# An earlier load of two head pairs and a later load of w_out in a fused cosine-attention and two-layer kernel

## The chip, the cores and the metric

The kernel runs on one core of a Trainium2 chip. The metric is the device time of one execution in microseconds (us): 413.31 us is the median of three runs of the kernel before the change, which lie between 413.31 and 413.9 us. The times of engines, waits and transfers come from one profiled execution of it, taken by the hardware profiler. The engines are called as in the profile: PE is TensorE (matrix products), DVE is VectorE, ACT is ScalarE, POOL is GpSimd, and SP is SyncE, which here only issues transfers (DMAs). POOL issues transfers too, on a queue of its own.

## What is computed

```python
q_n = q / (norm(q) + 1e-6);  k_n = k / (norm(k) + 1e-6)      # over the 64 channels of a head
attn = softmax(q_n @ k_n^T / tau)                            # per batch and head
o    = attn @ v                                              # q, k, v: [8, 12, 448, 64] float32
x    = o, with the 12 heads of a token side by side          # [3584, 768]
h    = x @ w_in;  g = max(0.01 * h, h)                       # w_in: [768, 2048]
out  = g @ w_out                                             # w_out: [2048, 768], out: [3584, 768]
```

The inputs and the output are float32 in memory; the matrix products run in bf16.

## The kernel before

**Pairs and quads.** Two heads of one batch are a *pair*; there are 6 pairs in a batch and 48 in all, numbered `s` from 0 (so the eleventh pair has number 10, and is called pair 10 here). Two pairs are a *quad* `j`, three in a batch. A pair goes through these steps, each of which is a function of the kernel:

- `load_qk(s)` (lines 135 to 147) issues four transfers on SP: the first 384 rows of q (L140), those of k (L141), and the last 64 rows of each (L143). The six pairs of the first batch have a tensor of their own, `raw0`; later pairs use one of four rotating buffers called `qk` (L139). A load can start only when the buffer's former pair has been read for the last time, which is the normalising of that pair.
- `squares(s)` (L180) squares q and k on POOL, `sums(s)` (L191) adds up each row on DVE, `roots(s)` (L198 and L199) takes the square root on ACT by logarithm and exponential, and `normalise(s)` (L215, L216, L220) divides and rounds to bf16 on DVE, into `qn`.
- `transposes(s)` brings channels onto partitions: by PE and a DVE copy (L258) for pairs 0 to 9, by a transposing DMA on SP (L252) from pair 10.
- `key_tiles` makes a tile of scores on PE (L277) and its exponential on ACT (L289), into `pe`, or `pr` for the 64 rows that are left over. Then `totals`, `products` and `scale` (L317, L336, L337, L358) form the attention output in `xT`.

`norm(s)` calls `roots`, `normalise` and `transposes` of pair `s`, issues the load of a later pair, and then puts `squares(s + 2)` on POOL. Ahead of the squares stands `hold` (L511), a tiny copy on POOL that reads the last part of `qn[s]`; it keeps POOL from going on before pair `s` is normalised.

**The two layers.** `first(c, m)` makes columns `m` of the first layer for a chunk of tokens (L381, 16 values of `m`) and ACT applies the leaky relu while it moves the result from its PSUM bank to `hT` (L388). `firsts(b, ...)` runs over all 16, with parts of the attention's preparation put between them. `visit(b, ...)` then makes the second layer of the same chunk (`groups`, L456) and, between its groups, the score tiles of the next batch, one tile at a time. A group is the two matmuls, on the two halves of the partitions, for one `m`. In the first visit (b = 0) two row tiles are worked on together in four parts of the 16 values of `m`: groups 1 to 16 need the first quarter of `w_out`, 17 to 32 the second, 33 to 48 the third, 49 to 64 the fourth. A second pass of 32 groups follows for the third row tile. The dictionaries `wide`, `three` and `four` say behind which group a score tile stands, and `norms` behind which group a pair's `sums` or `norm` stands.

**Order.** The order of the instructions on each engine is written out by hand: the program's order is the engine's order, and an instruction that waits holds up all that is behind it on its engine. There are eight PSUM banks, dealt out oldest first by `banks`; a matmul that is to write a bank waits until ACT or DVE has emptied it. The two queues that matter here are SP's (q1 in the profile, the loads of q and k, transposing DMAs and stores) and POOL's (q0, the loads of v, `w_in` and `w_out`, which round float32 to bf16 on the way). The weights are loaded in four parts each: `load_w_in(0..3)` (L106) and `load_w_out` (L112) for `m` from 0, 4, 8 and 12. They are issued from `bulk(s)` in the first batch, `w_out` right behind the last part of `w_in` and behind the squares of pair 7.

Around the change the program's order is: the attention of quad 2 (`attend(NQ - 1, ...)`, whose last step is `scale(2, 0)` and `scale(2, 1)` on DVE); `norm(6)` and `norm(7)`; `firsts(0, ...)` with `norm(8)`, `norm(9)`, the loads of v and `norm(10)` between its columns; `visit(0, ...)`, with `sums(11)` and `norm(11)` between its groups; and `attend_batch(1)`, which begins with the loads of pairs 14 and 15.

Of the kernel before, what the change touches and what calls it, by code (L numbers as in the profile page):

```python
# [8 lines left out]
F32 = mybir.dt.float32  # L9
# [7 lines left out]
def kernel(  # L17
# [10 lines left out]
    nc = tc.nc  # L28
    B, H, S, D = q.shape
# [9 lines left out]
    NQ = NPAIR // 2  # L39
# [11 lines left out]
    ldp = ctx.enter_context(tc.tile_pool(name="ld", bufs=4))  # L51
# [36 lines left out]
    def given_back(keep):  # L88
        deals["n"] += 1
        for i in kept.pop(keep):  # L90
            age[i] = deals["n"]
# [18 lines left out]
    def load_w_out(parts):  # L110
        for m in parts:
            gp.dma_start(out=w_out_sb[:, m : m + MT // 4], in_=w_out_r[:, m : m + MT // 4])  # L112

    def main(x, b, h0, nh):
        return x[b, h0 : h0 + nh, 0:MAIN].rearrange("h (p t) d -> p h t d", t=3)

    raw0 = cpool.tile([128, NPAIR, 2, 7, D], F32, name="raw0")
# [17 lines left out]
    def load_qk(s):  # L135
        if s >= NSLOT:
            return
        b, h0 = s // NPAIR, 2 * (s % NPAIR)
        both = ldp.tile([128, 2, 7, D], F32, name="qk")  # L139
        nc.sync.dma_start(out=both[:, :, 0:3], in_=main(q, b, h0, 2))  # L140
        nc.sync.dma_start(out=both[:, :, 4:7], in_=main(k, b, h0, 2))  # L141
        for i, x in enumerate((q, k)):
            nc.sync.dma_start(  # L143
                out=both[64 * i : 64 * i + 64, :, 3],
                in_=x[b, h0 : h0 + 2, MAIN:S].rearrange("h p d -> p h d"),
            )
        raw[s] = (both[:, :, 0:4], both[:, :, 4:7])
# [5 lines left out]
    def load_v(j):  # L153
        if j >= B * NQ:
            return
        b, jj = divmod(j, NQ)
        vb[j] = vbp.tile([128, 4, 3, D], BF16, name="v_b")
        gp.dma_start(out=vb[j], in_=main(v, b, 4 * jj, 4))  # L158
# [12 lines left out]
    def squares(s, engs=(gp, gp)):  # L171
        if s >= NSLOT:
            return
        tiles = []
        for x, eng, name in zip(raw[s], engs, ("sq0", "sq1")):
            sq = sqp.tile(list(x.shape), F32, name=name)
            if eng is nc.scalar:
                nc.scalar.activation(sq, x, func=AF.Square)
            else:
                eng.tensor_tensor(sq, x, x, op=ALU.mult)  # L180
            tiles.append(sq)
        sqs[s] = tiles

    def sums(s, parts=(0, 1)):
        if s >= NSLOT:
            return
        if s not in ss:
            ss[s] = smp.tile([128, 14], F32, name="ss")
        for i in parts:
            o = ss[s][:, 0:8] if i == 0 else ss[s][:, 8:14]  # L190
            nc.vector.tensor_reduce(  # L191
                o.rearrange("p (h t) -> p h t", h=2), sqs[s][i], axis=AX.X, op=ALU.add
            )
# [7 lines left out]
    qn, scalings = {}, {}  # L201

    def behind(eng, ins, why):

        tc.add_manual_dep(
            eng.nop().ins, ins.ins.name,
            mybir.DependencyInfo(mybir.DependencyClass.Sync, mybir.DependencyReason.DATA),
            reason=why,
        )
# [143 lines left out]
    def scale(j, e):  # L353
        b, jj = divmod(j, NQ)
        m, half = divmod(b, 2)
        if m not in xT:
            xT[m] = xtp.tile([128, KT, 2 * S], BF16, name="xT")
        nc.vector.tensor_tensor(  # L358
            xT[m][:, 2 * jj + e, half * S : (half + 1) * S], pos.pop((j, e))[:, :S], rbs[j],
            op=ALU.mult,  # L360
        )
        if (j, e) in kept:
            given_back((j, e))
# [3 lines left out]
    def chunk_cols(c):  # L367
        return (0, MAIN) if c % 2 == 0 else (MAIN, 512)
# [3 lines left out]
    def first(c, m, kts=range(KT)):  # L372

        c0, n = chunk_cols(c)
        if c not in hT:
            hT[c] = htp.tile([128, MT, 512], BF16, name="hT")
        if (c, m) not in pms:
            pms[c, m] = banks(1)
        pm = pms[c, m]
        for kt in kts:  # L380
            nc.tensor.matmul(  # L381
                out=pm[:, :n],
                lhsT=w_in_sb[:, kt, m * 128 : (m + 1) * 128],
                rhs=xT[c // 2][:, kt, c0 : c0 + n],
                start=(kt == 0), stop=(kt == KT - 1),
            )
        if kts[-1] == KT - 1:
            nc.scalar.activation(  # L388
                out=hT[c][:, m, :n], in_=pms.pop((c, m))[:, :n], func=AF.Prelu, alpha=0.01
            )  # L390
            if (c, m, 0) in kept:
                given_back((c, m, 0))
# [160 lines left out]
    def bulk(s):  # L553

        if s == 0:
            load_v(1)
            load_w_in(0)
        elif s == 1:
            load_v_rem(0, slice(2, 4))
            load_w_in(1)  # L560
        elif s == 2:
            load_v(2)
            load_w_in(2)
        elif s == 3:
            load_w_in(3)
            load_w_out((0, 4))
        elif s == 4:
            load_w_out((8, 12))

    def scaled(s):  # L570

# [81 lines left out]
    def attend(j, behind=()):  # L653
        totals(j)
        reciprocals(j)
        po = banks(2)
        for e in range(2):
            products(j, e, po[:, e])
        for fn in behind:
            fn()  # L660
        for e in range(2):
            scale(j, e)
# [30 lines left out]
    def norm(s, transposed=True):  # L693
        if s >= NSLOT:
            return
        roots(s)
        normalise(s)
        if transposed:
            transposes(s)
        if s == 10:  # L700
            return
        if s == 11:
            load_qk(12)
            load_qk(13)
        elif s not in (7, 8):
            load_qk(s + (2 if s == 9 else 4))
        hold(qn[s][:, 6, 0, 0:1])
        if s == 11:
            squares(12)
        squares(s + 2)  # L710

    def firsts(b, begun, between):

# [8 lines left out]
    def visit(b, order, norms, between):  # L722
# [14 lines left out]
        key_tiles([(s0 + 5, 3)])  # L737

    three = ({5: 1, 11: 1, 16: 2, 21: 1, 27: 1}, {3: 1, 7: 1, 11: 1, 16: 2, 20: 1})
    wide = (dict.fromkeys((5, 10, 16, 21, 26, 32, 37, 42, 48, 53, 58, 63), 1), three[1])  # L740
    four = ({5: 1, 11: 1, 16: 2, 24: 1}, {6: 1, 16: 2})

    deals["apart"] = False
    attend(NQ - 1, [lambda m=m: first(0, m, range(KT - 2)) for m in range(3, SOON)])
    norm(6, False)
    norm(7, False)
    firsts(
        0, SOON, {
# [11 lines left out]
    for b in range(B):  # L760
        tokens = chunk_cols(b)[1] // 128
        if b == B - 1:
            for ts in range(tokens):
                for half in range(2):
                    second(b, ts, half)
            break
        order = [[((ts, 0), (ts, 1))] for ts in range(tokens)]
        if b == 0:
            order = [order[0] + order[1], order[2]]
        norms = {(0, 16): [lambda: sums(11)], (0, 26): [lambda: norm(11)]}  # L770
        if b:
            norms = {}
            for i in range(tokens - 1):
                norms[i, 4] = [lambda s=ready + i: norm(s)]
                norms[i, 20] = [lambda s=ready + i + 1: sums(s)]
        visit(b, order, norms, wide if b == 0 else three if tokens == 3 else four)
        ready += tokens - 1
        attend_batch(b + 1)
        for j in range((b + 2) * NQ, (b + 3) * NQ):
            load_v(j)  # L780
        load_v_rem(b + 2)
        s = ready
        between = {0: [lambda s=s: norm(s)], 1: [lambda s=s: sums(s + 1)]}
        if b == 0:
            between = {
                0: [lambda: sums(13)], 1: [lambda: norm(13), lambda: sums(14)],
                4: [lambda: norm(14), lambda: sums(15)], 7: [lambda: norm(15)],
                13: [lambda: sums(16)],
            }
            ready += 4  # L790
        elif tokens == 3:
            between.update({
                4: [lambda s=s: norm(s + 1), lambda s=s: sums(s + 2)],
                7: [lambda s=s: norm(s + 2), lambda s=s: sums(s + 3)],
                10: [lambda s=s: norm(s + 3)], 13: [lambda s=s: sums(s + 4)],
            })
            ready += 4
        else:
            between.update({
                4: [lambda s=s: norm(s + 1)], 5: [lambda s=s: sums(s + 2)],  # L800
                8: [lambda s=s: norm(s + 2)], 12: [lambda s=s: sums(s + 3)],
            })
            ready += 3
        firsts(b + 1, 0, between)
# [35 lines left out]
```

## Time and profile before

| | us |
|---|---|
| device time, median of 3 runs | 413.31 |
| device time of the profiled execution | 413.39 |
| span of its instructions | 411.6 |
| PE busy | 402.1 |
| ACT busy | 263.4 |
| DVE busy | 189.6 |
| POOL busy | 139.0 |

The span is the time from the first to the last instruction on any engine; the 1.8 us between it and the device time lie before and after the instructions. "Busy" is time in which an engine had an instruction of the program in work. The profile cuts the span into 40 slices of 10.3 us each and prints the busy share of each engine as one digit, in tenths; the row PEclk is the clock that PE was granted, in tenths of its full speed. A wait is named as "engine line waited for", with its total, how often, and the longest one. In the rows by window the columns are the window, its length, and for each engine the busy time and the number of instructions, then the granted clock of PE (1.00 is full), the mean busy share of the 16 DMA engines (over 1 when transfers overlap), and GB/s.

### The profile page before, as it was taken

The numbers are of one execution on the slowest core, as the hardware profiler recorded it, in microseconds if no ns is written. First come the engines' busy times: TensorE is split into PE (matmuls) and PEld (weight loads), VectorE is DVE, ScalarE is ACT, GpSimd is POOL, SyncE is SP. The second block draws the span as 40 slices with busy tenths as digits, with TensorE's granted clock in tenths as the row PEclk, the third lists the DMA queues.
The fourth block names the chain that finished last, engine by engine and source line by source line (L and its number), as shares of the span: only waits on it lengthen the run. The fifth ranks groups of instructions, "written<-read, shape, count | busy, mean of one in ns | idle before, by whom it ended". The sixth has DMA issues, their size and how long they took to land.

```text
span 411.6 us, 10137 instructions
## 1 busy us (share of the span) xinstructions
PE 402.1 (98%) x4096; PEld 215.8 (52%) x4096; DVE 189.6 (46%) x405; ACT 263.4 (64%) x454; POOL 139.0 (34%) x212
## 2 busy tenths in 40 slices
PE   8999979999999999999999999999999999999996
PEld 3335546544555555544555555544555555554564
DVE  6887733573542635255352726157261544130021
ACT  4996468744876569845786469855776559844300
POOL 4992244283241514055140634054232530000000
PEclk9999989999999999999999999999999999999999
DMA  7999999599296948386387866575478832210023
GB/s 184 250 214 219 222 157 199 160 178 185 65 167 148 137 114 170 102 115 154 95 187 144 111 141 128 142 99 128 99 176 156 112 90 62 62 41 2 0 77 78
DMA packets 102095, 54.21 MB, mean 132 GB/s; under 512 B 69984, under 2 KB 96992, under 8 KB 102048
## 3 DMA queue, kind: packets, MB, share of 16 engines
q1 hardware_dynamic: 78064, 41.04, 43.4%
q0 software_dynamic: 23136, 12.00, 22.0%
q8 instruction: 32, 0.52, 0.6%
q10 hardware_dynamic: 848, 0.52, 0.4%
q14 instruction: 15, 0.12, 0.1%
HBM read 45.61 MB, written 11.01 MB: 138 GB/s over the span
## 4 chain that ended last, share of the span: by engine, by line
PE 88%; DMA 5%; DVE 2%; POOL 1%; issue 1%; ACT 1%; SPq 1%; POOLq 0%
PE ps L381 32%; PE ps L456 30%; PE ps L317 11%; PE ps L277 8%; PE ps L418 5%; DMA qk<-in_k_dram 3%; DMA raw<-in_q_dram 2%; PE ps L304 1%; DVE qn L220 1%; POOL sq L180 1%; DVE ss L191 0%; DVE r L216 0%; DVE xT L358 0%; ACT pe L289 0%; ACT pr L289 0%
## 5 line engine op out<-in xcount | busy, mean ns | idle before, releaser
L381 PE MATMUL ps<-xT,w_in_sb 128*128 128x384 bf16 (+1 forms) x768 | 148.2, 353 | 0.0
L456 PE MATMUL ps<-w_out_sb,hT 64*128 64x384 bf16 x1536 | 144.8, 325 | 2.1 <-ACT hT L388 2.1
L289 ACT ACTIVATE pe<-ps 128x896 bf16<-128x896 f32 x144 | 124.2, 918 | 21.0 <-PE ps L277 18.8
L388 ACT ACTIVATE hT<-ps 128x384 bf16<-128x384 f32 (+1 forms) x128 | 67.4, 543 | 70.4 <-PE ps L381 70.0
L381 PEld LDWEIGHTS <-w_in_sb 128*128 128x128 bf16 x768 | 74.0, 98 | 71.9 <-issue 4.0
L456 PEld LDWEIGHTS <-hT 64*128 64x128 bf16 x1536 | 75.4, 95 | 57.2 <-issue 5.2
L180 POOL TENSOR_TENSOR sq<-qk 128x512 f32<-128x512 f32 x84 | 77.3, 941 | 20.4 <-DMA qk<-in_k_dram 19.5
L191 DVE TENSOR_REDUCE ss<-sq 128x6 f32<-128x384 f32 (+1 forms) x95 | 54.6, 611 | 8.0 <-POOL sq L180 7.6
L277 PE MATMUL ps<-qkT 64*128 64x448 bf16 (+1 forms) x384 | 55.1, 356 | 2.2 <-ACT pe L289 0.8
L468 DVE COPY osb<-ps 128x384 f32<-128x384 f32 x41 | 21.2, 554 | 73.0 <-PE ps L456 42.5
L511 POOL CAST seen<-qn 128x1 f32<-128x1 bf16 x47 | 8.9, 189 | 130.5 <-DVE qn L220 123.9
L220 DVE TENSOR_TENSOR qn<-qk,r 128x512 bf16<-128x512 f32 x84 | 50.2, 639 | 1.7 <-DVE r L216 0.3
L215 DVE TENSOR_SCALAR ss<-ss 128x14 f32<-128x14 f32 x48 | 10.4, 216 | 68.2 <-ACT ss L199 68.1
L358 DVE TENSOR_TENSOR xT<-ps,rb 128x448 bf16<-128x448 f32 x48 | 27.8, 620 | 26.6 <-ACT rb L337 26.4
L158 POOL DMA_DIRECT2D v_b<-in_v_dram x24 | 18.6, 778 | 54.2 <-PE ps L317 54.2
L317 PE MATMUL ps<-pe,v_b 128*32 128x448 bf16 x576 | 32.0, 353 | 0.0
L277 PEld LDWEIGHTS <-qkT 64*128 64x128 bf16 (+1 forms) x384 | 16.7, 97 | 21.8 <-issue 9.4
L424 DVE COPY osb<-ps 128x384 f32<-128x384 f32 (+1 forms) x9 | 4.6, 514 | 36.5 <-issue 22.6
L336 ACT ACTIVATE rb<-ps 128x448 f32<-128x448 f32 x24 | 12.9, 538 | 13.2 <-PE ps L317 12.3
L317 PEld LDWEIGHTS <-v_b 128*32 128x32 bf16 x576 | 15.1, 97 | 12.0 <-issue 0.6
L289 ACT ACTIVATE pr<-ps 128x896 bf16<-128x896 f32 x24 | 21.2, 918 | 0.2 <-PE ps L277 0.2
L418 PE MATMUL ps<-w_out_sb,hT 128*128 128x384 bf16 (+1 forms) x144 | 21.0, 308 | 0.0
(49 smaller groups left out, 199.6 us busy)
## 6 DMA issues: line engine op xcount, KB each, us to landing
qk<-in_q_dram SPq DMA_DIRECT2D x42, 192.0 KB, 3.3
qk<-in_k_dram SPq DMA_DIRECT2D x42, 192.0 KB, 3.3
out_dram<-osb SPq DMA_DIRECT2D x30, 192.0 KB, 2.9
v_b<-in_v_dram POOLq DMA_DIRECT2D x24, 192.0 KB, 4.7
out_dram<-osb SPq DMA_DIRECT2D x12, 384.0 KB, 2.8
w_in_sb<-in_moe_w_in_dram POOLq DMA_DIRECT2D x4, 768.0 KB, 12.0
w_out_sb<-in_moe_w_out_dram POOLq DMA_DIRECT2D x4, 768.0 KB, 24.9
qk<-in_q_dram SPq DMA_DIRECT2D x42, 32.0 KB, 3.4
```

Source lines behind the costliest of these rows:

```text
L180: eng.tensor_tensor(sq, x, x, op=ALU.mult)
L191: nc.vector.tensor_reduce(o.rearrange("p (h t) -> p h t", h=2), sqs[s][i], axis=AX.X, op=ALU.add)
L220: scalings[s] = nc.vector.tensor_tensor(qn[s][:, lo:hi], x.rearrange("p h t d -> p t h d"), r[:, r0 : r0 + 2 * nt].rearrange("p (h t) -> p ...
L277: nc.tensor.matmul(out=out[:, a, :S], lhsT=x[rows, c0:c1], rhs=x[rows, 0:S], start=True, stop=True,)
L289: nc.scalar.activation(out=dst, in_=sc[:, :, :S], func=AF.Exp, scale=inv_tau)
L317: nc.tensor.matmul(out=x[32 * g : 32 * g + 32, :S], lhsT=weights(g, ki) if ki < 3 else rem(g), rhs=pe[s][:, ki, a, :] if ki < 3 else pr[j] ...
L358: nc.vector.tensor_tensor(xT[m][:, 2 * jj + e, half * S : (half + 1) * S], pos.pop((j, e))[:, :S], rbs[j], op=ALU.mult,)
L381: nc.tensor.matmul(out=pm[:, :n], lhsT=w_in_sb[:, kt, m * 128 : (m + 1) * 128], rhs=xT[c // 2][:, kt, c0 : c0 + n], start=(kt == 0), stop= ...
L388: nc.scalar.activation(out=hT[c][:, m, :n], in_=pms.pop((c, m))[:, :n], func=AF.Prelu, alpha=0.01)
L418: nc.tensor.matmul(out=po2[:, :n], lhsT=hT[c][:, m, ts * 128 : (ts + 1) * 128], rhs=w_out_sb[:, m, lo : lo + n], start=(m == 0), stop=(m = ...
L456: done[p][i] = nc.tensor.matmul(out=pos2[p][:, i, :HALF], lhsT=hT[c][rows, m, ts * 128 : (ts + 1) * 128], rhs=w_out_sb[rows, m, half * HAL ...
L468: copy(out=osb[c, ts][:, half * HALF : (half + 1) * HALF], in_=po2[:, i, :HALF])
```

## The change

Three things move; no operation is added to or taken from the computation.

1. Pairs 10 and 11 are loaded into the places of pairs 0 and 1 in `raw0`, in place of two of the rotating buffers. Both loads are issued on SP behind a wait for the first of the two scalings of quad 2. The loads of pairs 12 and 13 stay at `norm(11)`, and those of 14 and 15 at the attention of the next batch; they now take the rotating buffers of pairs 6 to 9.
2. The four parts of `w_out` leave `bulk`: two are issued by POOL behind the squares of pair 8 and two behind those of pair 9.
3. In the first visit the score tiles stand at other groups (11 in the first pass and 7 in the second, in place of 12 and 6), and `sums(11)` and `norm(11)` stand behind groups 8 and 18 in place of 16 and 26.

```diff
-        both = ldp.tile([128, 2, 7, D], F32, name="qk")
+        both = raw0[:, s - 10] if s in (10, 11) else ldp.tile([128, 2, 7, D], F32, name="qk")
...
-        nc.vector.tensor_tensor(
+        scalings[j, e] = nc.vector.tensor_tensor(
...
             load_w_in(3)
-            load_w_out((0, 4))
-        elif s == 4:
-            load_w_out((8, 12))
...
-        if s == 11:
-            load_qk(12)
-            load_qk(13)
-        elif s not in (7, 8):
-            load_qk(s + (2 if s == 9 else 4))
+        for x in (12, 13) if s == 11 else (s + 4,) if s > 11 else ():
+            load_qk(x)
         hold(qn[s][:, 6, 0, 0:1])
         if s == 11:
             squares(12)
         squares(s + 2)
+        if s in (6, 7):
+            load_w_out((0, 4) if s == 6 else (8, 12))
...
-    wide = (dict.fromkeys((5, 10, 16, 21, 26, 32, 37, 42, 48, 53, 58, 63), 1), three[1])
+    wide = (dict.fromkeys((5, 11, 16, 22, 27, 33, 38, 44, 49, 55, 60), 1), dict.fromkeys(range(4, 29, 4), 1))
...
     attend(NQ - 1, [lambda m=m: first(0, m, range(KT - 2)) for m in range(3, SOON)])
+    behind(nc.sync, scalings[NQ - 1, 0], "weights first")
+    load_qk(10)
+    load_qk(11)
     norm(6, False)
     norm(7, False)
...
-        norms = {(0, 16): [lambda: sums(11)], (0, 26): [lambda: norm(11)]}
+        norms = {(0, 8): [lambda: sums(11)], (0, 18): [lambda: norm(11)]}
```

`behind(engine, instruction, why)` makes the engine wait until that instruction of another engine has ended; `load_qk` and `load_w_out` are as described above.

## The prediction

> **What bounds the kernel now.** I read the page first: PE is busy in all but 9.5 us of the span, so only those microseconds, or a slower PE clock, can be won. In the slices the one hole far from both ends is the sixth digit of PE (51 to 62 us), with a lower PEclk below it.
>
> ```profile
> span 411.6 us, 10137 instructions
> PE 402.1 (98%) x4096; PEld 215.8 (52%) x4096; DVE 189.6 (46%) x405; ACT 263.4 (64%) x454; POOL 139.0 (34%) x212
> PE   8999979999999999999999999999999999999996
> PEclk9999989999999999999999999999999999999999
> ```
>
> PE's waits between 30 and 160 us name the hole; the windows price it. The first window is the first visit, from its first score tile to the next attention (L304); the second is the third visit, which has as many matmuls. The last shows PE's clock at half.
>
> ```profile
> PE ps L456 <- ACT hT L388: 2.1, 1, 2.1
> PE ps L277 <- ACT pr L289: 0.5, 1, 0.5
> PE ps L277 <- ACT pe L289: 0.3, 1, 0.3
> ```
>
> ```profile
> 50.56:75.62 25.06, 22.15 (x249) 13.32 (x256) 7.82 (x17) 19.11 (x26) 12.30 (x17) 0.93 1.02 178
> 150.39:170.32 19.93, 19.93 (x248) 11.20 (x256) 7.44 (x17) 18.35 (x26) 4.78 (x7) 1.00 0.60 121
> ...
> 55.00:56.00 1.00, 1.00 (x8) 0.53 (x6) 0.23 (x1) 1.00 (x2) 0.00 (x0) 0.50 1.17 202
> ```
>
> So the first visit has an excess of 25.06 - 19.93 = 5.13 us: waits of 2.1 + 0.47 + 0.34, and some 2.2 left for the half clock, which follows the wait from about 54.5 to 58.2. The chain that ended last says why ACT was late (start, us, what):
>
> ```profile
> 38.42 0.61 SPq L143
> ...
> 39.07 11.32 DMA qk<-in_k_dram
> ...
> 51.55 0.84 POOL sq L180
> ...
> 52.41 0.56 DVE ss L191
> ...
> 53.00 0.32 ACT ss L198
> 53.32 0.02 issue
> 53.34 0.21 ACT ss L199
> 53.56 0.38 ACT hT L388
> ```
>
> Pair 10's last piece needs 11.32 us to land (50.4); squares, sums and roots follow. The roots stand on ACT ahead of the last relu, whose bank PE needs at 51.88. Last, the transfers. Here are POOL's issues of w_out and its squares (start, us, what), then the packets, MB and engine share of each queue from 42 to 44 us; from 40 to 42 us, nearly without SP's; and from 68 to 69 us, SP's alone.
>
> ```profile
> 26.21 1.52 POOL L112 DMA_DIRECT2D w_out_sb<-in_moe_w_out_dram  x2
> 29.65 1.55 POOL L112 DMA_DIRECT2D w_out_sb<-in_moe_w_out_dram  x2
> 38.13 2.38 POOL L180 TENSOR_TENSOR sq<-qk 128x512 f32<-128x512 f32 x2 [0.38 <-POOL seen L511]
> 41.59 1.82 POOL L180 TENSOR_TENSOR sq<-qk 128x512 f32<-128x512 f32 x2 [0.95 <-DMA qk<-in_k_dram]
> ```
>
> ```profile
> q0 software_dynamic: 210, 0.30, 83.3%
> q1 hardware_dynamic: 211, 0.15, 30.6%
> ...
> q0 software_dynamic: 240, 0.37, 101.0%
> ...
> q1 hardware_dynamic: 380, 0.27, 108.3%
> ```
>
> The queues take turns packet by packet (210 and 211), and POOL's are bigger; so beside weights SP gets 0.075 MB/us, alone 0.27. The weights occupy q0 until about 58 us.
>
> **Part 1, loads 10 and 11 at quad 2's scaling.** In the trace SP issues load 10 at 37.49 (after pair 6's normalising) and load 11 at 39.88. The new wait ends with the scaling that starts at 34.71, at about 35.3: two and four microseconds earlier. By itself that is worth nothing: load 9 has the SP queue until it lands at 41.43, and the order in it stays. Behind the waiting SP instruction stand only these eight issues and then the transposing DMAs of pairs 10 and 11, which before go at 55.39 and 64.08; nobody else waits. The places of pairs 0 and 1 were last read by 20 us. Load 11's last pieces still wait, as before (1.52 us of issue at 41.52), until load 9's pieces have landed. Loads 12 to 15 only get buffers that are free longer.
>
> **Part 2, w_out behind the squares of pairs 8 and 9.** POOL gives back 1.52 us at 26.21 and 1.55 at 29.65; it then waits for pair 6 until 37.56 anyway, so the path gains nothing there. The issues move to 40.5 (end of pair 8's squares) and, with pair 9's squares pushed to 42.2 to 44.1, to 44.1. These squares are summed at 44.88, so the push is covered by 0.8 us. Pair 10's squares can begin at about 45.8. w_in's last part lands at 40.5 (issued 25.40, 15.1 us), and a v load issued at 60.00 has its packets from about 62.0; so for at least 2 us, 40.5 to 42.5, SP has the DMA engines alone. It moves 2 x 0.27 = 0.54 MB, more than load 10's 0.46. Load 10 lands at 43 to 45 in place of 50.4. Load 11, with the rest at 0.075 MB/us, takes (0.92 - 0.54) / 0.075 = 5.1 us more: 48 to 50 in place of 58.1 (53 if SP alone were no faster than half of 0.27).
>
> Then the chain is: squares 45.8 to 47.7; DVE has copies until 49.35 (48.20 + 1.15) and sums pair 10 by 50.7 (1.34); roots 0.56 and relu 0.38 end at 51.6, before PE asks at 51.88. The 2.1 us go, and with them the half clock, 2.2. Next late is the first pr exponential: 0.82 after the relu, 52.4, where PE asks at 52.05. I leave the whole 0.47 wait in.
>
> The price is w_out's arrival. In the trace its parts land at 46.3, 50.6, 55.8 and 59.9 (issues plus 20.1, 23.6, 26.2 and 29.4). PE will need part k at 51.06 + 16k x 0.163 + 0.19 for each score tile passed + 0.45: 51.1, 54.6, 57.7, 60.8. From below: if the engines do the same work in the same time, only in another order, all is there at 59.9 and PE waits 0. From above: the two queues apart need 0.54/0.27 = 2.0 us, then 0.38 MB of loads beside 0.76 of w_out at 0.225 MB/us = 5.1, then the other 2.39 MB at 0.185 = 12.9; 20.0 us where the mix took 4.07/0.225 = 18.1. That is 1.9 late: 61.8; and pair 10's transposing DMA, now ahead of the last part, can add up to 1.5 (143.9% of the engines in the us from 57): 63.3, a wait of 2.5. I take 0.7, nearer the lower end, because the lower end is the row of the same packets and engines.
>
> The page "SBUF — State Buffer" of the Trainium skill (section "SBUF: two separate sides") speaks against the move: descriptors that POOL writes stall while some DVE operations hold a shared port. The trace: w_out's issues at 26 to 31 us took 0.76 us each with DVE busy 1.00, v's at 60.0 0.77 with DVE at 0.5; but a v load landed after 5.7 us at 14.13 and 4.6 at 60.00. By the rule w_out would be 1 us later and the sum 410.4; by the issue rows it is unchanged.
>
> **Part 3, tiles and norm(11).** The number of tiles stays 18, so PE and ACT have the same work. In the steady visits, 18 tiles, three pr and a relu fit ACT (18.35 of 19.93); tiles every four groups in the second pass (4 x 0.163 + 0.19 = 0.84 against 0.86 an exponential) lag by some tenths, covered by the 5.79 us of L317 before the last are read. The 0.34 us wait at 68.3 goes with the wider spacing; if it stays, 0.3 is lost. ACT reaches roots(11) at 51.6 + 5 x 0.87 = 56.0; its sums come 2.6 us after load 11 lands (58.07 to 60.64 before), so at about 53, hidden. The cover is gone from a landing at 53.4 on. norm(11) before the rest only moves loads 12 and 13 ahead (65.4 to about 60); squares 12 wait behind the v loads as before and are read past 75 us.
>
> **Sum**, against the profiled execution's 413.39 (0.08 over the median): 413.39 - 5.13 + 0.47 + 0.7 = 409.43; on the median 409.4.
>
> **Rivals.**
> - *w_out is late by more.* For: its queue starts about 2 us (up to 4) later. Wait of 1.5 to 2.5: 410.2 to 411.2.
> - *Slower: a w_out wait that halves PE's clock again.* At the third or fourth quarter one wait of over about 2 us (2.1 did it; 0.47 did not) costs itself and 2.2 again. With 0.47, it decides at 2.5 us: 5.13 - 0.47 - 2.2. Every us beyond is lost: w_out's last part past 63.3, 3.4 later than before, would do; at 64.3 the wait of 3.5 gives 409.4 + 2.8 + 2.2 = 414.4. Against: that lies past my upper bound. The page "TensorE: Matmul & The Clock Gate" of the Trainium skill (section "What's actually happening") puts the gate at an idle window of about 3.4 us. This trace halves after 2.1, so the measurement decides; by the rule a wait of 3.3 would cost only itself and give 412.0.
> - *The clash moves to roots(11).* If load 11 lands past 53.4, ACT stands at roots(11), 8 groups earlier than before, and the tile at group 33 waits for its bank (0.65 us of slack). At 56 the sums come at 58.6, roots and one exponential 1.4 later, 2.0 after the tile asks: 411.4. Against: SP's time alone.
> - *The change does not do what it says:* no time alone for SP, pair 10 lands at 50 as before: 413.3.
>
> **How the numbers follow.** Forecast (w_out wait below 1.5: 408.2 to 410.2) 0.69; w_out late by more 0.11; roots(11) 0.07, a fifth of it no gain; no effect 0.04; slower 0.09, a little of it within 0.2%. 0.2% (0.8 us) is about what a measurement of this kernel can tell from no change. Faster 0.86, same 0.05, slower 0.09. The range runs from 408.2 (all 5.13 gone, no new wait) to 411.5, the end of the late w_out.
>
> **What would show it.** Right: w_out issued near 40.5 and 44; load 10 landing before 46, load 11 before 53; no L456 wait on hT; PEclk full at 51 to 62 us; the first visit 20 to 22 us. A wait of L456 on w_out is the price. Wrong: L388 still late, a long ACT wait at L198, or a second half-clock stretch.

## The result, and the profile after

The changed kernel takes 409.37 us (median of 4 runs, 408.64 to 409.56) against 413.46 us before (413.31 to 413.9 beside it): a ratio of 0.9896, 95% interval 0.9879 to 0.9913. The forecast was 409.4. The profiled execution took 409.41 us with a span of 407.6. As will be seen, the mechanism was the one forecast, but that the total fits this closely is partly luck: two terms were too high by about 1 us together, and that was made up by 0.6 us and some pauses that stood in no term. One part of the change was judged wrongly.

The page of the changed kernel, the same rows as before: the hole at 51 to 62 us and the clock's dip below it are gone.

```profile
span 407.6 us, 10141 instructions
PE 399.9 (98%) x4096; PEld 215.1 (53%) x4096; DVE 189.6 (47%) x405; ACT 263.1 (65%) x454; POOL 138.7 (34%) x212
PE   7999999999999999999999999999999999999996
PEclk9999999999999999999999999999999999999999
```

PE's waits between 30 and 160 us are down to one, and the windows show the stretch before the visit and the first visit (51.16 to 71.66), each with 0.2 us of idle time of PE left:

```profile
PE ps L277 <- ACT pr L289: 0.2, 1, 0.2
```

```profile
34.94:51.16 16.22, 16.00 (x116) 9.60 (x112) 15.08 (x28) 8.37 (x23) 11.54 (x17) 1.00 1.10 220
51.16:71.66 20.50, 20.33 (x249) 13.00 (x249) 6.39 (x15) 18.70 (x26) 7.91 (x12) 1.00 1.22 209
```

The visit is 25.06 - 20.50 = 4.56 us shorter, and begins 51.16 - 50.56 = 0.60 us later: 3.96 us in all, and the span fell by 4.0. Now the transfers. The first rows are load 10's four pieces in the changed kernel with their time to landing (issued from 35.43 to 37.17, so landed by 42.4, before 50.4); then the packets of the two queues from 40 to 42 us and from 48 to 50 us:

```profile
raw<-in_q_dram SPq DMA_DIRECT2D x1, 192.0 KB, 6.1
raw<-in_k_dram SPq DMA_DIRECT2D x1, 192.0 KB, 6.1
raw<-in_q_dram SPq DMA_DIRECT2D x1, 32.0 KB, 5.7
raw<-in_k_dram SPq DMA_DIRECT2D x1, 32.0 KB, 5.2
...
q1 hardware_dynamic: 806, 0.48, 78.9%
q0 software_dynamic: 12, 0.02, 13.8%
...
q0 software_dynamic: 275, 0.42, 116.0%
```

From 40 to 42 us SP had the engines almost to itself (806 packets, 0.48 MB); from 48 to 50 us w_out had them, and moved 0.42 MB. POOL issued w_out at 39.99 and 43.46 (start, us, what), and the parts landed between 7.8 and 15.1 us after their issue, the last at 59.3:

```profile
39.99 1.56 POOL L112 DMA_DIRECT2D w_out_sb<-in_moe_w_out_dram  x2
...
43.46 1.56 POOL L112 DMA_DIRECT2D w_out_sb<-in_moe_w_out_dram  x2
```

### The profile page after: what moved, and what is told of

Its sections match the earlier page's. It is cut to its first block, busy times and chain, and to the rows that moved or that the text cites. A ratio compares the mean times of both kernels' runs of the same rounds, so it can differ in the third digit from the quotient of the medians.

```text
span 407.6 us, 10141 instructions
## 1 busy us (share of the span) xinstructions
PE 399.9 (98%) x4096; PEld 215.1 (53%) x4096; DVE 189.6 (47%) x405; ACT 263.1 (65%) x454; POOL 138.7 (34%) x212
## 4 chain that ended last, share of the span: by engine, by line
PE 88%; DVE 5%; POOL 2%; ACT 1%; DMA 1%; issue 1%; POOLq 0%
PE ps L381 33%; PE ps L456 31%; PE ps L317 11%; PE ps L277 8%; PE ps L418 5%; DVE qn L220 2%; PE ps L304 1%; POOL sq L180 1%; DMA raw<-in_k_dram 1%; DVE ss L191 1%; DVE ss L215 1%; DVE qkT L258 1%; DVE r L216 0%; POOL raw L130 0%; POOL v_rem L165 0%
## 5 line engine op out<-in xcount | busy, mean ns | idle before, releaser
L180 POOL TENSOR_TENSOR sq<-qk 128x512 f32<-128x512 f32 x80 | 73.4, 938 | 10.7 <-DMA qk<-in_k_dram 10.1
L220 DVE TENSOR_TENSOR qn<-qk,r 128x512 bf16<-128x512 f32 x80 | 48.2, 644 | 1.7 <-DVE r L216 0.3
L215 DVE TENSOR_SCALAR ss<-ss 128x14 f32<-128x14 f32 x48 | 10.5, 220 | 69.2 <-ACT ss L199 69.1
```

What stands on the lines that cost most here:

```text
L220: scalings[s] = nc.vector.tensor_tensor(qn[s][:, lo:hi], x.rearrange("p h t d -> p t h d"), r[:, r0 : r0 + 2 * nt].rearrange("p (h t) -> p ...
```

## The experiments

Three questions were open after the result. Which of the three parts makes the gain? What does the half clock cost, apart from the wait that sets it off? And why does PE enter the first visit 0.6 us later? The theory at the start was the prediction's: the later w_out frees pair 10, the earlier load does nothing by itself, and the moved tiles cost nothing once load 11 is early. In what follows the length of the first visit is taken from the start of its first score tile to the start of the first L304, both from the timeline; it is 24.99 us in the kernel before and 20.43 in the changed one. It leaves out when PE enters the visit, which varies from execution to execution.

### One part at a time

**The later w_out alone** (kernel before plus)

```diff
             load_w_in(3)
-            load_w_out((0, 4))
-        elif s == 4:
-            load_w_out((8, 12))
...
         squares(s + 2)
+        if s in (6, 7):
+            load_w_out((0, 4) if s == 6 else (8, 12))
```

> The kernel before with the later issue of w_out alone; pairs 10 and 11 are loaded as before. Theory (the gap in POOL's queue is what frees pair 10): SP's transfers have the engines alone from about 38.5 to 42.5 us, load 10 lands before 46 us, the wait of L456 on hT and the half clock are gone, and nearly the whole gain is there: 409 to 410.2 us. Rival (the earlier load is needed): load 10 still lands near 50 us and the time stays near 413.4.

Measured: 410.19 us (409.78 to 410.76), ratio 0.9930 (0.9902 to 0.9958). Load 10, issued from 38.30 on, landed by 42.3; the wait on hT and the half clock are gone. The theory held. The time is 0.8 us over that of the full change: the visit takes 20.81 us, and in the profiled run PE entered it 0.4 us later, after a wait of 0.8 us for w_in's last part. A wait of 0.3 for pe stayed, as before.

**The earlier loads alone** (kernel before plus)

```diff
-        both = ldp.tile([128, 2, 7, D], F32, name="qk")
+        both = raw0[:, s - 10] if s in (10, 11) else ldp.tile([128, 2, 7, D], F32, name="qk")
...
+    behind(nc.sync, scalings[NQ - 1, 0], "weights first")
+    load_qk(10)
+    load_qk(11)
     norm(6, False)
```

> The kernel before with the earlier loads of pairs 10 and 11 alone; w_out is issued as before. Theory: load 9 and the weights hold the queues, load 10 lands near 50 us as before, 413 to 413.7 us. Rival (the earlier issue frees pair 10): load 10 lands some 2.4 us earlier, the wait of L456 shrinks below 0.5 us, the clock stays full and the time is 409 to 411.

Measured: 410.52 us (410.38 to 410.75), ratio 0.9936 (0.9915 to 0.9957). The theory fell: this part alone is worth 3.0 us. Its waits of PE, and its packets from 40 to 42 us:

```profile
PE ps L381 <- DMA w_in_sb<-in_moe_w_in_dram: 0.7, 1, 0.7
PE ps L456 <- ACT hT L388: 0.5, 1, 0.5
PE ps L277 <- ACT pr L289: 0.5, 1, 0.5
PE ps L277 <- ACT pe L289: 0.3, 1, 0.3
```

```profile
q0 software_dynamic: 199, 0.30, 82.9%
q1 hardware_dynamic: 203, 0.15, 30.2%
```

In the kernel before, the same 2 us show 240 packets of w_out and only 94 of SP's, and 17 of those in the first of the two: load 9 had all but run out, and load 10, asked for from 37.49 on, was hardly flowing. With the earlier issue SP takes its turn there (203 packets), and load 10 lands at 49.3 in place of 50.4. PE itself came to the visit 0.54 us later, after the wait for w_in, so the 1.1 us were enough to bring its wait on hT from 2.1 to 0.5 us. The clock stayed at 1.00 after that. The waits listed went from 2.1 + 0.47 + 0.34 to 0.5 + 0.5 + 0.3, and the half clock went: the visit took 21.75 us (from 51.10 to 72.85).

**The moved tiles, sums(11) and norm(11) alone** (kernel before plus)

```diff
-    wide = (dict.fromkeys((5, 10, 16, 21, 26, 32, 37, 42, 48, 53, 58, 63), 1), three[1])
+    wide = (dict.fromkeys((5, 11, 16, 22, 27, 33, 38, 44, 49, 55, 60), 1), dict.fromkeys(range(4, 29, 4), 1))
...
-        norms = {(0, 16): [lambda: sums(11)], (0, 26): [lambda: norm(11)]}
+        norms = {(0, 8): [lambda: sums(11)], (0, 18): [lambda: norm(11)]}
```

> The kernel before with the moved score tiles, sums(11) and norm(11) alone. Theory: load 11 lands at 58 us as before, its sums come at 60.6, and ACT now reaches roots(11) some 3 us earlier and stands there; the tiles behind it are late and PE waits 0.5 to 2 us more for pe: 413.8 to 415.5. Rival (ACT's backlog is covered by the two free tile buffers): 413.2 to 413.6, or less by the 0.34 us wait on pe at 68.3.

Measured: 415.22 us (413.12 to 417.37, 10 runs), ratio 1.0038 (1.001 to 1.0066): a little slower, as the theory has it, though the runs scatter widely. In the profiled run, 416.21 us, load 11 landed late, ACT came to roots(11) early and stood there 2.90 us, PE waited 2.1 us for pe, and the clock fell after that second wait. ACT's rows (start, us, what, idle before):

```profile
56.26 2.85 ACT L289 ACTIVATE pe<-ps 128x896 bf16<-128x896 f32 x3
62.01 0.31 ACT L198 ACTIVATE ss<-ss,tiny 128x14 f32<-128x14 f32 x1 [2.90 <-DVE ss L191]
```

```profile
PE ps L456 <- ACT hT L388: 2.2, 1, 2.2
PE ps L277 <- ACT pe L289: 2.1, 1, 2.1
```

**Both other parts, without the moved tiles.** The edits of the first two runs together.

> The changed kernel with the old positions of the tiles, sums(11) and norm(11). Theory: the new positions do little once load 11 is early; 409.2 to 409.9. Rival (the wider spacing is what takes away the waits on pe in the second half of the visit): two or more waits of L277 on pe, 410 to 411.

Measured: 409.88 us (409.85 to 410.38), ratio 0.9924 (0.9897 to 0.9951). This is inside the theory's range, at its upper end. One wait on pe of 0.3 us stays, and the visit takes 20.81 us where the full change takes 20.43. The moved tiles are worth about 0.4 us once load 11 is early.

**The later w_out and the moved tiles, without the earlier loads.**

> The changed kernel without the earlier loads: pairs 10 and 11 go to the rotating buffers as before. Theory: load 11 is issued at 40 us, the gap in POOL's queue is long enough for it, and the time is that of the changed kernel within 0.5 us: 409.0 to 409.9. Rival: load 11 is late, ACT stands at roots(11), 410 to 412.

Measured: 409.23 us (408.78 to 410.6), ratio 0.9897 (0.9875 to 0.9919): the changed kernel's time. Load 11 landed by 51.2 (47.6 in the changed kernel), which is early enough. The visit takes 20.43 us here too, and 20.81 in both kernels with the old tiles and the later w_out. So beside the later w_out the earlier loads are worth nothing that can be measured, and beside the old w_out they are worth 3.0 us: each of the two takes away the same wait, and the second finds little left. The earlier loads and the moved tiles without the later w_out were not run.

### How much later w_out may come

```diff
-        if s in (6, 7):
-            load_w_out((0, 4) if s == 6 else (8, 12))
+        if s == 7:
+            load_w_out((0, 4, 8, 12))
```

> The changed kernel with all four parts of w_out issued behind the squares of pair 9, at about 43.5 us: the first two parts 3.5 us later than in the changed kernel. It measures what margin is left. In the changed kernel the last part lands at 59.3 and is needed near 61.3. Theory (POOL's queue alone moves 0.21 MB/us, so four parts take 15 us and the slowest engine 1.5 more): the last part lands at 61.5 to 63, PE waits 0.2 to 1.7 us on it: 409.6 to 411.1. Rival (the order of the queues does not matter, all transfers end near 59.9): no wait, 409.2 to 409.6.

Measured: 411.11 us (410.66 to 411.38), ratio 0.9936 (0.9921 to 0.9951), 1.7 us over the changed kernel. The rival that the prediction set beside its forecast is real, and begins here:

```profile
PE ps L456 <- DMA w_out_sb<-in_moe_w_out_dram: 1.6, 1, 1.6
PE ps L277 <- ACT pr L289: 0.2, 1, 0.2
```

The first two parts were issued 2.6 us later than in the changed kernel and the last two 0.6 to 0.7 later. The last was issued at 44.88 and landed 17.9 us later, at 62.8. A wait of 1.6 puts the need at about 61.2; in the changed kernel it landed at 59.3. The margin of the change was about 1.9 us.

### What the half clock costs

**Matmuls in the wait of the kernel before**, between groups 4 and 5, into the one bank of the group that is already free:

```diff
+                if c == 0 and x == 0 and p == 1 and len(pairs) > 1:
+                    free = 1 - (last_bank[0] - pos_at[1])
+                    for i in range(9):
+                        nc.tensor.matmul(out=pos2[1][:, free], lhsT=warm[:, :128], rhs=warm, ...)
```

> The kernel before with 9 matmuls of 512 columns on constants (about 1.9 us of PE, results overwritten) put between groups 4 and 5 of the first visit, where PE waits 2.1 us for the last relu. They begin no later than the wait and fill it. Theory (the half clock is the price of that idle time): PEclk stays full from 51 to 62 us and the time falls by about 2.2 us, to 411 to 411.6, though the pair is as late as before. Rival (the clock falls for another reason, or the wait alone costs the 5.1 us): 413 to 414.

Measured: 412.81 us (411.79 to 413.49, 10 runs), ratio 0.9978 (0.9965 to 0.9991). PEclk stayed at 1.00, as the theory has it, but the time fell by 0.8 us and not by 2.2. The profile shows one reason: with the clock full, ACT came to roots(11) earlier than load 11 allowed, stood 1.31 us, and PE waited 1.0 us for pe (0.34 before). The half clock had been covering 0.7 us of waiting. With the 0.8 gained that makes about 1.5 us, still not 2.2: the half-clock stretch of the kernel before lasted 3.4 us (its mean clock from 54 to 59 us is 0.66), and 3.4 us at half speed can cost 1.7 at most.

**The clock by itself.** In the changed kernel pair 11 is early, so nothing waits for it. Three activations ahead of the last relu bring the wait back:

```diff
         if kts[-1] == KT - 1:
+            for _ in range(3 if (c, m) == (0, MT - 1) else 0):
+                nc.scalar.activation(idle, raw0[:, 2], func=AF.Square)
             nc.scalar.activation(
```

> The changed kernel with three activations of 128x896 (about 2.5 us of ACT, results unused) put ahead of the last relu of the first chunk, so that PE again waits about 2.1 us between groups 4 and 5, while pairs 10 and 11 are early. Theory (a wait of that length halves PE's clock for about 4 us, which costs 2 us more): L456 waits 1.9 to 2.3 us on hT, PEclk falls to 0.5, and the time is 4 to 5 us over the changed kernel: 413.2 to 414.4. Rival (in the kernel before the half clock was one-off or harmless): 411.3 to 412.2.

The same with the nine matmuls in the wait:

> The run before with 9 matmuls of 512 columns on constants (1.9 us of PE, results overwritten) in the wait. Theory: the relu is as late, but PEclk stays full, and the time is 1.7 to 2.5 us below the run before: 411.2 to 412.2. Rival (ACT's delay, not the clock, makes the price): within 0.5 us of the run before.

Measured: 413.77 us (413.09 to 415.2, 10 runs) with the idle wait, 412.27 us (411.72 to 412.51, 8 runs) with the matmuls in it; the ranges do not meet. 1.5 us between the medians is the price of the clock; at least 1.7 was expected. The mean clock of each run tells how long the half clock lasted. Seven idle runs have 0.994 to 0.996, much like the kernel before with its stretch of 3.4 us; their median, 413.57 us, is 1.3 over that of the runs with matmuls. Three have 0.991, so about twice that stretch, and a median of 414.91, 2.6 over it. The profiled run is one of the three. PE waited 2.3 us, and the clock by window shows the fall near the end of the wait and the half clock for 6.8 us:

```profile
53.00:54.00 1.00, 0.00 (x0) 0.00 (x0) 1.00 (x3) 0.97 (x2) 1.00 (x3) 1.00 1.18 214
54.00:55.00 1.00, 0.21 (x2) 0.10 (x2) 0.29 (x1) 1.00 (x3) 1.00 (x2) 0.66 1.14 204
...
60.00:61.00 1.00, 1.00 (x10) 0.51 (x6) 0.00 (x0) 0.54 (x1) 0.00 (x0) 0.50 1.46 180
61.00:62.00 1.00, 1.00 (x15) 0.55 (x12) 0.15 (x1) 0.78 (x3) 0.00 (x0) 0.93 1.64 186
```

### The 0.6 us before the visit

In the changed kernel the chain that ended last no longer runs through a load. From 37.84 us on it runs along DVE and the roots on ACT, from the normalising of pair 7 through those of pairs 8 and 9 to the first leftover tile (start, us, what):

```profile
37.84 2.62 DVE qn L220 x2
...
42.14 1.43 DVE ss L215
...
43.87 1.16 DVE qn L220 x2
...
47.72 1.16 DVE qn L220 x2
...
51.97 0.82 ACT pr L289
...
52.83 0.36 PE ps L277 x2
```

PE loses the 0.60 us at two places of that chain, the transposes of pairs 8 and 9 (L234). Up to 44.7 us it is as early as before. Here are these transposes and the first score tile, in the kernel before and in the changed one:

```profile
44.66 0.55 PE L234 MATMUL ps<-id,qn 128*128 128x128 bf16 x7
...
47.98 0.70 PE L234 MATMUL ps<-id,qn 128*128 128x128 bf16 x7
...
50.56 0.57 PE L277 MATMUL ps<-qkT 64*64 64x448 bf16 x8
```

```profile
44.68 0.74 PE L234 MATMUL ps<-id,qn 128*128 128x128 bf16 x7
...
48.47 0.81 PE L234 MATMUL ps<-id,qn 128*128 128x128 bf16 x7
...
51.16 0.57 PE L277 MATMUL ps<-qkT 64*64 64x448 bf16 x8
```

The normalising of pairs 8 and 9 ends at 45.03 and 48.88 us, 0.60 later than before. Two DVE operations ahead of it are longer, each while POOL's squares run: the normalising of pair 7 takes 2.62 us in place of 2.00, and the tiny L215 of pair 8 takes 1.42 in place of 0.95. The rows of the changed kernel (start, us, what):

```profile
37.84 2.62 DVE L220 TENSOR_TENSOR qn<-qk,r 128x512 bf16<-128x512 f32 x2
...
42.14 1.42 DVE L215 TENSOR_SCALAR ss<-ss 128x14 f32<-128x14 f32 x1
```

The first of the two belongs to the later w_out. In all eight profiles with w_out moved and these squares in place, POOL's squares of pair 8 begin 0.06 us ahead of the normalising of pair 7, and it takes 2.62 or 2.63 us. In all four with the early w_out, the squares begin 0.3 us behind it, and it takes 2.00. Why POOL begins earlier there is not shown. The length of L215 changes from execution to execution: in a second profile of the changed kernel it took 0.64 us, and PE lost only 0.2 us to this chain.

The experiment moves the squares of pair 8 to where POOL is idle:

```diff
         bulk(s)
+        if s == 4:
+            squares(8)
...
-        squares(s + 2)
-        if s in (6, 7):
-            load_w_out((0, 4) if s == 6 else (8, 12))
+        if s == 7:
+            load_w_out((0, 4))
+        if s != 6:
+            squares(s + 2)
+        if s == 7:
+            load_w_out((8, 12))
```

> The changed kernel with the squares of pair 8 right behind those of pair 7 on POOL, where POOL was idle from 29 to 37.6 us; the first two parts of w_out are issued behind the hold on pair 7, near 39 us. In the changed kernel PE entered the first visit 0.6 us later than before. Theory (POOL's squares of pair 8 ran beside DVE's normalising of pair 7, which took 2.62 us in place of 2.00, and the transposes waited): with these squares gone from there, DVE's normalising takes about 1.2 us, PE enters the visit at 50.6, and the time falls by 0.4 to 0.7: 408.6 to 409.0. Rival (the 0.6 us come from POOL's later squares of pair 9 holding up pair 8's normalising): no change beyond 0.2 us.

Measured: 408.91 us (408.56 to 409.26), ratio 0.9884 (0.9867 to 0.9901). Pair 7's normalising takes 1.16 us and the visit begins at 50.64, though L215 took 1.48 us. PE waited for no part of w_in in this profile or in the changed kernel's first one, so the 0.52 us between them come from the DVE chain. The same kernel and the changed kernel were run once more side by side:

> The changed kernel once more, on the chip of the other runs of this call, to stand beside the next one: 409.0 to 409.7.

> The changed kernel with the squares of pair 8 behind those of pair 7, once more beside the changed kernel. Theory (POOL's squares beside DVE's normalising make PE enter the first visit late): 0.3 to 0.6 us below the changed kernel, visit entered at 50.6 against 51.2. Rival (the late entry comes and goes from run to run, with the landing of w_in's last part): no difference over 0.2 us.

Measured: the changed kernel 409.51 us (409.02 to 409.74), ratio 0.9903 (0.9887 to 0.9919); with the early squares 408.87 us (408.67 to 409.04), ratio 0.9889 (0.9874 to 0.9905). The two ranges touch at 409.02 to 409.04, and the visit begins at 51.38 and at 50.72. This is the fastest version here, by about 0.5 us. Not all of that is the overlap. In both profiles PE waits for w_in's last part, which lands between 40.05 and 41.1 us from execution to execution: 0.9 us in the second profile of the changed kernel, 0.4 in the one beside it. At the transposes of pair 6 PE is therefore 0.32 us apart in the two (38.66 and 38.34), and at the visit 0.66: in these two executions half of the difference is the landing, and half the DVE chain. How the other executions divide isn't shown.

## Why the prediction was right, and where it was not

**The excess of the first visit, 5.13 us, as the sum's base.** Right within 0.1: it is what there was to win, and all but 0.57 of it went. (It is 0.07 too high, and so is the 0.57: the start, 50.56, was read from the timeline and the end, 75.62, from the chain, which has the same L304 0.07 later than the timeline.)

**Part 1, "by itself that is worth nothing".** Wrong. It was argued from the order of the queue (load 9 lands at 41.43, so an earlier issue cannot help), while the row of 40 to 42 us, quoted as the price of w_out "nearly without SP's", showed SP's queue running dry: 94 packets against 240. The earlier loads alone gave 410.52. That it did no harm to the sum is luck: part 2 takes away the same wait.

**Part 2, SP alone for some 2 us.** Right, and a little better than priced: load 10 landed at 42.4 (43 to 45 forecast) and load 11 at 47.6 (48 to 50), with the squares of pair 10 from 45.37 to 47.2 (45.8 to 47.7). The wait on hT and the half clock went, as worked out. The end of the chain was less right: the relu ended at 51.97 where 51.6 was forecast, and did not hold PE only because PE came late as well.

**The price, w_out's arrival: 0.7 us.** Mis-sized: it measured 0. The last part landed at 59.3, a little before the prediction's lower end (59.9, the same work in another order). The upper end took w_out alone at 0.185 MB/us from a row in which SP still had 94 packets; alone it moved 0.42 MB in 2 us, 0.21. The mechanism itself is there, about 1.9 us further on.

**The pr wait, 0.47 left in.** As the profile lists it, it measured 0.17: the exponential ended at 52.78 and not at 52.4, but PE came 0.6 us later to it. By the starts of the matmuls the pause is 0.34 us, and another of 0.15 stands at 67.7; these two make up the 0.50 that stayed in the visit by the timeline.

**What was not in the sum: PE's late entry, 0.60 us.** The prediction took the end of DVE's copies for pair 9, 49.35, from the kernel before; it came at 49.95. It called the push of pair 9's squares covered because the sums behind them were late enough, and did not ask what POOL's squares do to a DVE instruction that runs beside them. So 0.47 + 0.7 = 1.17 was forecast to stay, and 0.57 + 0.60 = 1.17 did, out of other pieces. That the two sums agree is luck.

**The half clock, 2.2 us.** Too high, because it was what the listed waits left over. The stretch lasted 3.4 us, so it can hold 1.7 at most; the pauses are longer by the starts of the matmuls than the waits that the profile lists (2.26 where it lists 2.1). As a price of its own the half clock is 1.5 us in the pair of runs made for it and 0.8 in the kernel before, where a later wait was hidden under it.

**The rivals.** The late w_out exists (411.11 when its last part lands 3.5 us later), the clash at roots(11) exists (415.22 when load 11 stays late), and neither was reached by the change. The wait of 1.6 us on w_out left the clock full, so the slower rival's second half-clock stretch would have needed more still. The Trainium skill's page "SBUF — State Buffer" (section "Who interferes with whom") says that a DVE operation with two SBUF inputs contends with a POOL operation that reads SBUF, and that the later one waits in full. The trace agrees: 1.16 us for the two L220 alone, 2.00 where they began 0.3 us ahead of POOL's squares, 2.62 where they began 0.06 behind. The prediction had drawn on that page for the descriptors only, where the issues stayed at 0.78 us each and no lateness showed.

## What to carry to other kernels

When two queues take turns, look for the moments in which one of them has nothing to send: load 10, asked for at 37.49 us, had next to nothing in flight from 40 to 41, when its turn had come. A long wait of PE can be ended by any of several small gains, so two edits that win 3.4 and 3.0 us alone won 3.7 together here; only undoing them one at a time shows it. Moving an operation to a time when its own consumer is late enough is not free if it holds up another engine at that time. And when a wait is gone, follow the chain that ends last anew: here it had moved from a load to DVE's normalising, where the next 0.5 us lay.

## What was not expected of the hardware

- A wait of PE of about 2.1 us halves its clock in most executions, not in all: of the 46 runs of the kernel before that stand beside the experiments, 10 kept a granted clock of 1.0 (411.37 to 413.76 us), and 36 had 0.994 to 0.996 (412.92 to 414.23). The profiled run with the moved tiles alone shows a wait of 2.2 us without a fall. Waits of 0.5 and 1.6 us left it alone. The half clock lasted 3.4 us in the profiles of the kernel before and of the moved tiles, and 6.8 in that of the idle wait. The page "TensorE: Matmul & The Clock Gate" of the Trainium skill (section "What's actually happening") has a free-running window of 3.4 us; free-running fits the chance, and 3.4 and 6.8 us are one and two such windows, while the 2.1 us lie below the length that it gives.
- A DVE operation on 128x14 values, 0.17 us by itself, took up to 1.48 us when it was issued beside POOL's squares of 128x512 and 128x384. What holds up so small an operation, with one input, isn't shown.
- The landing of w_in's last part varied from 40.05 to 41.1 us between executions of nearly equal kernels, and cost PE up to 1.1 us.
